# Sixty-two more unread TensorE products, of 128 columns, ahead of the transposes and values of units 1 to 3

## The chip, the cores and the metric

The kernel runs on one core of a Trainium2 chip. The metric is the device time of one execution in microseconds; lower is better. The times before are those of three runs.

## The reference

Sliding-window attention over 8 batches and 8 heads (576 positions, 64 numbers a head, window of 32 to each side), then a feed-forward layer with a quick gelu, all given and returned as float32:

```python
q, k, v: (8, 8, 576, 64);  w_in: (512, 2048);  w_out: (2048, 512)

scores = (1 / sqrt(64)) * q @ k.T
scores = where(abs(i - j) <= 32, scores, -1e9)
attn   = exp(scores - rowmax);  attn = attn / (rowsum + 1e-9)
x      = (attn @ v)            # heads side by side: (4608, 512)
h      = x @ w_in
out    = (h * sigmoid(1.702 * h)) @ w_out      # (4608, 512)
```

## The kernel before

The 4608 tokens are cut into 36 *units* of 128 tokens and 9 *tiles* of 512 (four units). For a unit, `scores` multiplies the transposed q and k of all heads into two banks of PSUM, ScalarE takes the exponential into `p`, VectorE multiplies it by the band mask (`band`), `values` multiplies `p` by v with a column of ones beside it into `pv`, and `norm` divides by the sum that this column gives and writes `x`. `x_T` and `x_T2` transpose `x` on TensorE, for one unit and for two, and copy the result into `xT`, the moving operand of layer one. Layer one (`h`) is 16 groups of products a tile with a gelu each, layer two (`o`) follows; from tile 1 on both use seven products of sums of blocks in place of eight, whose sums VectorE makes (`x_sums`, line 354, and `g_sums`).

Everything is recorded in an order written out by hand, one queue an engine; the engines wait for one another by semaphores that the framework sets from the tiles used. `opening` holds the order for the first tiles. It begins with tile 0: q and k of the first batch come in two parts and are transposed on TensorE by `T_first`, then units 0 and 1 go through scores, band, values and norm, and their `x` is transposed by two calls of `x_T` (lines 614 and 616). The second part of k is transposed (line 617), layer one of the first half of tile 0 begins (`layer1_plain`, lines 625, 627, 632 and 633, eight products of 256 columns each), with the second part of q and the scores of units 2 and 3 in between. `self.do(gelus)` records four gelus on ScalarE. Then come the bands, the values and norms of units 2 and 3 (lines 636 to 641) and `x_T2(2, "A", dve)`, line 642, which transposes both.

PSUM banks go by tags: "t" is a pair of banks, "A", "B", "C", "E", "LA" and "LB" one each. A new use of a tag waits until the readers of its last use are done.

`keep_busy(n, tag, cols=256)` records `n` products of an all-zero tile with itself, of `cols` columns, into the bank `tag`; no instruction reads the result. Each product is two TensorE instructions, a weight load and the product. In the profile they are `junk<-idle`. The kernel calls it in six places of the opening, with 256 columns, two of them (lines 613 and 615) ahead of the transposes of units 0 and 1. In the profile every product that `mm` records has line L70.

Of the kernel before, what the change touches and what calls it, by code (L numbers as in the profile page):

```python
# [26 lines left out]
class _Kernel:  # L27
# [534 lines left out]
    def opening(self):  # L562

        nc, dve, act, pool = self.nc, self.nc.vector, self.nc.scalar, self.nc.gpsimd
        self.setup()
        dve.memset(self.idle, 0.0)
        dve.memset(self.spark, 0.0)
        for t in self.ve:
            dve.memset(t[:, :, self.D:], 1.0)
        self.load_first("k", 0)  # L570
        self.load_first("q", 0)
        make_identity(nc, self.ident)
        act.activation(self.spark, self.spark, AF.Exp)
        for u in (0, 1, 2):
            self.load_v(u)
        self.load_w1(0)
        self.setup_mask()
        self.load_first("k", 1)
        self.load_first("q", 1)
        self.cut_mask()  # L580
        self.load_w1(1)
        self.load_v(3)
        self.load_v(4)
        self.load_w1(2)
        self.load_four("k")
        self.load_four("q")
        self.load_w1(3)
        dve.tensor_copy(self.identh, self.ident)
        self.keep_busy(20, "E")
        self.T_first("k", 0, "AC", (dve, act))  # L590
        self.keep_busy(6, "E")
        self.T_first("q", 0, ("LA", "LB"), (dve, act))
        self.keep_busy(4, "E")
        for u in (5, 6):
            self.load_v(u)
        self.load_w2(0)
        for u in (7, 8):
            self.load_v(u)
        for c in (1, 2, 3):
            self.load_w2(c)  # L600
        self.load_kq("k", 8)
        self.scores(0, "t")
        self.scores(1, "AC")
        self.odd_v(0, dve)
        self.odd_v(1, dve)
        self.keep_busy(10, "E")
        self.band(0)
        self.band(1)
        self.values(0, "t")
        self.values(1, "AC")  # L610
        self.norm(0)
        self.norm(1)
        self.keep_busy(6, "E")
        self.x_T(0, "LA", act)
        self.keep_busy(4, "E")
        self.x_T(1, "LB", act)
        self.T_first("k", 1, "AC", (dve, dve))
        h, n, gelus = [], [0], []

        def l1(half, *ds):  # L620
            for d in ds:
                self.layer1_plain(0, d, half, h[n[0] % len(h)])
                n[0] += 1

        self.layer1_plain(0, 0, 0, "B", gelus)
        self.T_first("q", 1, ("LA", "LB"), (dve, act))
        self.layer1_plain(0, 1, 0, "E", gelus)
        self.odd_v(2, dve)
        self.odd_v(3, dve)
        h[:] = ["LB", "B", "E"]  # L630
        self.scores(2, "t")
        self.scores(3, "AC")
        self.layer1_plain(0, 2, 0, "LA", gelus)
        self.layer1_plain(0, 3, 0, "LB", gelus)
        self.do(gelus)
        self.band(2)
        self.band(3)
        self.values(2, "t")
        self.norm(2)
        self.values(3, "AC")  # L640
        self.norm(3)
        self.x_T2(2, "A", dve)
        l1(0, 4)
        dve.tensor_copy(self.k_first, self.kT[0][:, :, 0:64])
        dve.tensor_copy(self.v_first, self.ve[0][0:64])
        for u in (8, 9, 10, 11):
            self.fetch(u)
        l1(1, 0, 1)
        halo = self.kT[4]
        self.T_four("k", "AC", (dve, dve))  # L650
        dve.tensor_copy(self.kT[4][:, :, 0:64], halo)
        l1(1, 2, 3)
        l1(0, 5)
        self.T_four("q", "AC", (dve, act))
        l1(1, 4, 5)
        self.odd_v(4, dve)
        self.scores(4, "t")
        self.scores(5, "AC")
        for i in (3, 1, 2, 4):
            self.w1_sums((i,), 0)  # L660
        self.odd_v(5, dve)
        for d, tag in ((6, "B"), (7, "E")):
            self.layer1_plain(0, d, 0, tag, gelus)
        self.do(self.l2, 3)
        self.scores(6, "t")
        self.do(self.l2, 3)
        self.scores(7, "AC")
        self.do(gelus)
        self.do(self.l2, 2)
        self.band(4)  # L670
        self.band(5)
        self.odd_v(6, dve)
        self.odd_v(7, dve)
        self.band(6)
        self.values(4, "t")
        self.norm(4)
        self.band(7)
        self.values(5, "AC")
        self.norm(5)
        self.do(self.l2, 8)  # L680
        self.values(6, "t")
        self.norm(6)
        self.values(7, "AC")
        self.norm(7)
        h[:] = "BE"
        n[0] = 0
        for i in (3, 1):
            self.w1_sums((i,), 1)
        l1(1, 6, 7)
        self.x_T2(4, "A", act)  # L690
        self.do(self.l2, 4)
        self.x_T2(6, "t", dve)
        self.do(self.l2, 4)
# [214 lines left out]
```

## Time and profile before

| what | value |
|---|---|
| median of three runs | 288.69 us (288.52 to 289.27) |
| span of the profiled execution, first to last instruction | 287.4 us |
| the median less the span | 1.3 us |
| instructions | 9107 |
| TensorE busy, products and their weight loads | 274.7 us, 3762 of each |
| granted TensorE clock, mean | 1.000 |
| DMA read and written | 36.83 MB, 9.44 MB |

The execution that was profiled has no time of its own among the three runs; what is worked out from its rows is set against its span, and the 1.3 us outside the span are taken as fixed. Busy time of TensorE counts products as they overlap; two products that follow each other closely each show the full time from start to end, so the step from one start to the next is what a product costs. A line of the timeline gives the start, the time from the first start to the last end, engine, line, operation, output and inputs, the count, and in brackets the idle time ahead of it and what ended it. In a row of the table of stretches, the numbers are: stretch, its length, busy time and count of products (PE), of weight loads (PEld), then of VectorE, ScalarE and GpSimd, the granted clock, the busy share of the DMA engines and the GB/s.

### The profile page before, as it was taken

The numbers are of one execution on the slowest core, as the hardware profiler recorded it, in microseconds if no ns is written. First come the engines' busy times: TensorE is split into PE (matmuls) and PEld (weight loads), VectorE is DVE, ScalarE is ACT, GpSimd is POOL, SyncE is SP. The second block draws the span as 40 slices with busy tenths as digits, with TensorE's granted clock in tenths as the row PEclk, the third lists the DMA queues.
The fourth block names the chain that finished last, engine by engine and source line by source line (L and its number), as shares of the span: only waits on it lengthen the run. The fifth ranks groups of instructions, "written<-read, shape, count | busy, mean of one in ns | idle before, by whom it ended". The sixth has DMA issues, their size and how long they took to land.

```text
span 287.4 us, 9107 instructions
## 1 busy us (share of the span) xinstructions
PE 274.7 (96%) x3762; PEld 227.1 (79%) x3762; DVE 216.9 (75%) x501; ACT 194.0 (68%) x340; POOL 127.3 (44%) x192
## 2 busy tenths in 40 slices
PE   7878999999999997999999999999999999999995
PEld 5666857776777885888788888888888888888884
DVE  1756898897887975798779887988797878946731
ACT  2455784789787767676967696679668965558421
POOL 8964448798599746456345826360210000000000
PEclk9999999999999999999999999999999999999999
DMA  8999999999999999999999999998432150401023
GB/s 94 186 192 197 184 204 156 190 116 140 168 141 148 175 142 173 138 203 144 188 97 181 161 168 105 173 135 146 95 77 45 69 112 0 94 2 73 2 92 130
DMA packets 148074, 37.63 MB, mean 131 GB/s; under 512 B 134976, under 2 KB 143680, under 8 KB 148032
## 3 DMA queue, kind: packets, MB, share of 16 engines
q0 software_dynamic: 104464, 18.42, 92.3%
q1 hardware_dynamic: 43120, 18.10, 36.0%
q8 instruction: 29, 0.48, 0.7%
q10 hardware_dynamic: 448, 0.52, 0.6%
q14 instruction: 13, 0.11, 0.1%
HBM read 36.83 MB, written 9.44 MB: 161 GB/s over the span
## 4 chain that ended last, share of the span: by engine, by line
PE 81%; DMA 5%; DVE 5%; ACT 3%; POOL 2%; issue 2%; DVEq 0%; ACTq 0%; POOLq 0%
PE h L70 38%; PE o L70 34%; PE pv L70 3%; DMA xT<-x 3%; PE sc L70 2%; DMA kq<-in_k_dram 2%; DVE x L294 2%; ACT p L256 1%; PE tp L322 1%; POOL ve L199 1%; ACT L256 1%; DVE p L264 1%; PE tp L189 1%; PE tp L232 1%; ACT g L419 1%
## 5 line engine op out<-in xcount | busy, mean ns | idle before, releaser
L419 ACT ACTIVATE g<-h 128x512 f16<-128x512 f32 x128 | 72.1, 598 | 35.8 <-PE h L70 35.0
L70 PEld LDWEIGHTS <-g 128*128 128x128 f16 x576 | 54.4, 98 | 11.4 <-issue 1.8
L70 PEld LDWEIGHTS <-a 128*128 128x128 f16 x512 | 49.1, 97 | 12.7 <-DVE xs L354 2.1
L70 PE MATMUL h<-xs,a 128*128 128x256 f16 x384 | 57.6, 272 | 1.2 <-DVE xs L354 0.9
L70 PE MATMUL o<-w,g 128*128 128x256 f16 (+1 forms) x320 | 55.3, 294 | 0.9 <-issue 0.8
L70 PEld LDWEIGHTS <-w 128*128 128x128 f16 x512 | 49.1, 98 | 7.8 <-issue 1.2
L70 PE MATMUL h<-xT,w 128*128 128x256 f16 x384 | 54.0, 273 | 1.1 <-issue 1.0
L199 POOL DMA_DIRECT2D ve<-in_v_dram x40 | 34.0, 855 | 40.7 <-issue 33.7
L70 PEld LDWEIGHTS <-gs 128*128 128x128 f16 x384 | 36.8, 98 | 5.2 <-issue 0.4
L256 ACT ACTIVATE p<-sc 128x512 bf16<-128x512 f32 x72 | 36.6, 619 | 3.2 <-PE sc L70 3.2
L70 PE MATMUL o<-b,gs 128*128 128x256 f16 x256 | 37.8, 273 | 1.0 <-issue 0.5
L70 PE MATMUL o<-b,g 128*128 128x256 f16 x256 | 37.3, 273 | 0.0
L432 DVE TENSOR_TENSOR h<-h,s 128x512 f32<-128x512 f32 x32 | 22.3, 698 | 18.2 <-PE h L70 18.2
L131 POOL DMA_DIRECT2D qst<-in_q_dram x35 | 28.1, 805 | 5.5 <-DMA w<-in_moe_w_out_dram 3.2
L131 POOL DMA_DIRECT2D kst<-in_k_dram x31 | 26.4, 854 | 8.5 <-DMA ve<-in_v_dram 2.6
L67 ACT COPY h<-h 128x512 f32<-128x512 f32 x32 | 18.6, 581 | 16.6 <-PE h L70 16.2
L294 DVE TENSOR_TENSOR x<-pv,rec 128x256 f16<-128x256 f32 (+1 forms) x53 | 27.6, 520 | 1.8
L438 DVE TENSOR_TENSOR h<-h,s 128x512 f32<-128x512 f32 x32 | 22.4, 700 | 5.1 <-PE h L70 4.6
L264 DVE TENSOR_TENSOR p<-p,mask 128x1024 bf16<-128x1024 bf16 x36 | 24.6, 685 | 0.9 <-ACT p L256 0.8
L209 POOL COPY vo<-ve 64x264 int32<-64x264 int32 x28 | 13.4, 480 | 24.9 <-PE pv L70 23.8
L67 ACT COPY s<-h 128x512 f32<-128x512 f32 x32 | 19.1, 596 | 3.0 <-PE h L70 1.8
L70 PE MATMUL h<-xs,w 128*128 128x256 f16 x128 | 19.2, 273 | 0.0
(85 smaller groups left out, 361.1 us busy)
## 6 DMA issues: line engine op xcount, KB each, us to landing
out_dram<-o_sb SPq DMA_DIRECT2D x33, 256.0 KB, 3.9
ve<-in_v_dram POOLq DMA_DIRECT2D x32, 128.0 KB, 6.3
kst<-in_k_dram POOLq DMA_DIRECT2D x25, 128.0 KB, 6.8
qst<-in_q_dram POOLq DMA_DIRECT2D x21, 128.0 KB, 6.1
w<-in_moe_w_in_dram POOLq DMA_DIRECT2D x4, 512.0 KB, 8.9
w<-in_moe_w_out_dram POOLq DMA_DIRECT2D x4, 512.0 KB, 13.4
qst<-in_q_dram POOLq DMA_DIRECT2D x7, 96.0 KB, 5.5
kq<-in_q_dram POOLq DMA_DIRECT2D x2, 256.0 KB, 5.9
```

The source lines that it names most:

```text
L67: (eng.copy if eng is self.nc.scalar else eng.tensor_copy)(out, in_)
L70: self.nc.tensor.matmul(out, lhsT, rhs, start=start, stop=stop, skip_group_check=True)
L131: self.nc.gpsimd.dma_start(t[off:off + n], src[b, :, s:s + n, :].rearrange("h s d -> s h d"))
L189: self.nc.tensor.transpose(tp[64 * (h % 2):64 * (h % 2) + 64, h // 2, j, :], src[:, 4 * i + h, j, :], self.ident)
L199: self.nc.gpsimd.dma_start(t[off:off + n, :, :self.D], self.v[b, :, s:s + n, :].rearrange("h s d -> s h d"))
L209: eng.tensor_copy(words(vo[64:128]), words(self.ve[u % 9][64:128]))
L256: self.nc.scalar.activation(p[:, eo].rearrange("k h s -> k (h s)"), sc[eo], AF.Exp, scale=self.scale)
L264: (eng or self.nc.vector).tensor_mul(pv, pv, msk.to_broadcast([128, 8, 2, SQ]))
L294: dve.tensor_mul(x[:, 4 * at:4 * (at + n), :].rearrange("p (b h) d -> p b h d", b=n), acc[:, :, :, :D], r.to_broadcast([128, n, 4, D]))
L419: act.activation(g[:, f, 256 * half:256 * half + 256], bank.rearrange("p (i n) -> p i n", i=2), AF.Gelu_apprx_sigmoid)
L432: dve.tensor_add(e, b, s7)
L438: dve.tensor_add(c, b, s7)
```

## The change

Two calls of `keep_busy` ahead of the transposes of units 0 and 1 take 12 and 8 products of 128 columns in place of 6 and 4 of 256. Three calls are new: 12 products ahead of the transposes of the second part of k, 20 ahead of the values of unit 2, into the banks of tag "t", and 20 ahead of the transposes of units 2 and 3, into bank "B". That is 72 products of 128 columns in place of 10 of 256. Nothing that is read changes.

```diff
         self.norm(0)
         self.norm(1)
-        self.keep_busy(6, "E")
+        self.keep_busy(12, "E", 128)
         self.x_T(0, "LA", act)
-        self.keep_busy(4, "E")
+        self.keep_busy(8, "E", 128)
         self.x_T(1, "LB", act)
+        self.keep_busy(12, "E", 128)
         self.T_first("k", 1, "AC", (dve, dve))
...
         self.do(gelus)
         self.band(2)
         self.band(3)
+        self.keep_busy(20, "t", 128)
         self.values(2, "t")
         self.norm(2)
         self.values(3, "AC")
         self.norm(3)
+        self.keep_busy(20, "B", 128)
         self.x_T2(2, "A", dve)
         l1(0, 4)
```

## The prediction

> **What bounds the kernel now.** I read the page's busy row first, then the chain of waits of the whole span, then TensorE's waits in the opening, then the timeline of the stretch that the change touches.
>
> ```profile
> PE 274.7 (96%) x3762; PEld 227.1 (79%) x3762; DVE 216.9 (75%) x501; ACT 194.0 (68%) x340; POOL 127.3 (44%) x192
> PE 81%; DMA 5%; DVE 5%; ACT 3%; POOL 2%; issue 2%; DVEq 0%; ACTq 0%; POOLq 0%
> ```
>
> TensorE is busy for 96% of the span and carries 81% of the chain. From 24 us on hardly any idle time stands between its products, so microseconds lost in the opening should be paid at the end too. TensorE's waits up to 30 us are these, the largest first:
>
> ```profile
> PE junk L70 <- DVE spark L567: 1.3, 1, 1.3
> PE tp L322 <- DVE x L294: 1.1, 1, 1.1
> PE h L70 <- issue: 1.0, 1, 1.0
> PE pv L70 <- DVE p L264: 1.0, 2, 0.5
> PE tp L168 <- DMA kq<-in_k_dram: 0.9, 2, 0.5
> ```
>
> Only 1.1 us (the transposes of units 2 and 3) and half of the last row (the second k transposes) are waits that the added products can stand in. The third row, "issue", is 1.0 us in which TensorE waited for nothing that the profile shows. TensorE's timeline, with the mask products and exponentials that feed the values of units 2 and 3 (the values lines left out):
>
> ```profile
> 1.27 4.26 PE L70 MATMUL junk<-idle 128*128 128x256 bf16 x20 [1.27 <-DVE spark L567]
> ...
> 12.47 0.83 PE L70 MATMUL junk<-idle 128*128 128x256 bf16 x6
> 13.14 0.39 PE L310 MATMUL tp<-identh,x 128*128 128x128 f16 x4
> 13.36 0.60 PE L70 MATMUL junk<-idle 128*128 128x256 bf16 x4
> 13.80 0.52 PE L310 MATMUL tp<-identh,x 128*128 128x128 f16 x4
> 14.86 0.71 PE L168 MATMUL tp<-ident,kq 64*64 64x64 bf16 x32 [0.54 <-DMA kq<-in_k_dram]
> 15.51 1.05 PE L70 MATMUL h<-xT,w 128*128 128x256 f16 x8
> ...
> 18.11 0.70 PE L70 MATMUL sc<-kq 64*64 64x64 bf16 x48
> 18.74 1.48 PE L70 MATMUL h<-xT,w 128*128 128x256 f16 x12
> 21.24 0.60 PE L70 MATMUL h<-xT,w 128*128 128x256 f16 x4 [1.02 <-issue]
> 21.77 0.22 PE L70 MATMUL pv<-ve,p 128*64 128x65 bf16 x1
> ...
> 23.82 0.83 PE L322 MATMUL tp<-identh,x 128*128 128x128 f16 x8 [1.08 <-DVE x L294]
> 18.60 2.07 ACT L256 ACTIVATE p<-sc 128x512 bf16<-128x512 f32 x4 [0.78 <-PE sc L70]
> 20.96 1.27 DVE L264 TENSOR_TENSOR p<-p,mask 128x1024 bf16<-128x1024 bf16 x2
> ```
>
> Twelve of sixteen layer-one products run, then TensorE stands from 20.22 to 21.24 in the middle of a group, its data and bank there. I read this as TensorE out of instructions, for this reason. The counts of products and weight loads up to that stall and up to the two later "issue" stalls of 0.8 and 0.5 us (109.65 and 139.52 us), in the table of stretches; the counts are in the third and fourth columns' brackets:
>
> ```profile
> 0.00:15.07 15.07, 11.93 (x223) 8.96 (x224) 6.57 (x26) 6.00 (x10) 13.52 (x29) 1.00 1.24 143
> 0.00:18.48 18.48, 15.34 (x327) 11.74 (x329) 8.84 (x30) 6.59 (x11) 15.14 (x31) 1.00 1.32 150
> 0.00:20.50 20.50, 17.08 (x350) 13.14 (x351) 9.51 (x33) 8.48 (x15) 16.38 (x33) 1.00 1.34 155
> 20.50:109.90 89.40, 85.52 (x1273) 65.25 (x1272) 73.42 (x157) 68.08 (x119) 63.59 (x87) 1.00 1.93 162
> 109.90:139.80 29.90, 28.03 (x382) 23.55 (x383) 23.44 (x55) 20.65 (x37) 17.06 (x25) 1.00 2.04 168
> 34.14:40.08 5.94, 5.71 (x147) 3.81 (x135) 5.60 (x13) 5.89 (x11) 2.82 (x4) 1.00 1.49 195
> 104.52:109.65 5.13, 5.13 (x130) 4.00 (x127) 4.06 (x10) 4.99 (x9) 4.20 (x6) 1.00 2.02 130
> ```
>
> First stall after 350 + 351 = 701; then 2545 to the second and 765 to the third, which is ten and three times 256 less 15 and 3; I put the missing few down to separate wait instructions in TensorE's list, which these columns leave out. So stalls come only at every 256th instruction. Within each such block one packet of queue 8 is read, and in the block before the first stall it falls between 18.7 and 19.8 us:
>
> ```profile
> q8 instruction: 1, 0.02, 5.7%
> ```
>
> That block begins near count 701 - 256 = 445, at about 15.07 us (447 begun by then); the next may start only at 21.24. So from beginning one block to being allowed into the next takes about 21.24 - 15.07 = 6.17 us here. A block used up sooner ends in a stall: the one from 104.52 was used in 5.13 us and was followed by 0.8 us of idling (5.94 in all). [...]
>
> **The change part by part.** A 128-column product costs 55 ns: four transposes of that width start at 13.14 and the next work at 13.36. One of 256 columns costs (13.14 - 12.47) / 6 = 112 ns. Only TensorE's list grows, by 124 instructions (62 products and their loads); the other engines' lists and all DMA issues stand in the same order.
>
> *Ahead of unit 0's and unit 1's transposes:* 12 narrow for 6 wide, 12 x 55 = 0.66 against 0.67 us; 8 for 4, 0.44 against 0.44. Nothing; 20 more instructions.
>
> *Ahead of the second k transposes:* 12 x 55 = 0.66 us. Unit 1's transposes leave TensorE at about 14.16, the k rows arrive at 14.86: 0.70 us of cover. Nothing, with 0.04 us to spare, 24 more instructions. Without that cover it costs 0.66.
>
> *The stall.* These 44 instructions stand before it. The block that begins at count 445 now begins inside the twelve new products, at about 14.27 instead of 15.07; adding 6.17, the next block is allowed at 20.4. But the 701st instruction is now what was the 657th, in the middle of unit 3's scores, which TensorE reaches at 18.48 (327 + 329 = 656 begun). So TensorE stands from about 18.5 to 20.4, 1.9 us, in place of 1.2 (from 20.06, where the next product was due at 109 ns steps, to 21.24). Bounds for the restart: 18.5 if the reading of blocks is wrong or the block comes at once, 21.24 if the fetch keeps its old hour because the DMA queues are what delays it. I take 20.4, the row's own round trip.
>
> *Ahead of the values of unit 2:* 20 x 55 = 1.1 us. Now the rest: from 18.48 to unit 2's values the old trace has 0.26 of scores, 1.32 for twelve products and 0.53 for four, 2.11 us. 20.4 + 2.11 + 1.1 = 23.6, against 21.77: **+1.85 us**. The wait that these products could have stood in, for the mask product (the first ends near 21.6), is already over by 22.5. Behind them queue the values of both units, then reciprocals and normalisations on VectorE, the transposes and layer one. Unit 3's exponentials come after the stall, near 20.7 to 21.8, and its mask product by 22.5, still ahead of 23.6; the gelus slip by 1 us and are done by 25.2, before their banks are wanted near 26.3.
>
> *Ahead of units 2's and 3's transposes:* 20 x 55 = 1.1 us in the wait of 1.08 us, which moves along with the values: about nothing (0 to 0.1), since bank B's gelu is over by then. Without that cover, 1.1.
>
> *Later.* With 124 more instructions every later block begins 124 earlier in the program. The stall at 139.52 is in TensorE's own run of work, so its going gives -0.5. The one at 109.65 gives nothing: the chain through it is a DMA transpose, and TensorE waits for its result 2 us later anyhow:
>
> ```profile
> 103.43 8.78 DMA xT<-x
> PE h L70 <- DVE xs L354: 0.9, 1, 0.9
> ```
>
> New stalls: at the moved places the shortest block I find after the opening is that of 34.14 to 40.08, 5.94 us (the row's 282 counts products in flight at the edges), against 5.7 to 6.2: 0 to 0.3. I take 0.
>
> *Sum:* +1.85 - 0.5 = +1.3 us. The profiled span is 287.4 us and the median of the timed runs 288.69, so 1.3 us lie outside the span and are left as they are: 288.69 + 1.3 = **290.0 us**. About 0.3%, 0.9 us, is what a measurement of this kernel can tell from no change.
>
> **The rivals.** *No stall in the opening* (0.16): the next block is there by 18.5. Then layer one ends near 20.6, the twenty products fill the wait for the mask product until about 21.7, and nothing is lost; with the 0.5 won later, 288.2, and 287.4 if the 0.8 us counts too. For it: the block of 104.52 came after 5.94 us, so the trip is not fixed at 6.17. Against it: three stalls, all on the 256 grid. It decides if the round trip is below 18.75 - 14.27 = 4.5 us.
>
> *Bare products* (0.12): the stall is no matter of blocks and stays as large, 1.0 to 1.2 us, at the same product, and nothing changes later; the twenty before unit 2's values lie open: +1.1, 289.8.
>
> *The fetch keeps its hour* (0.13): restart at 21.24, so 21.24 + 2.11 + 1.1 - 21.77 = +2.7, less 0.5: 290.9.
>
> *Swallowed downstream* (0.12): loads and DMA transposes do not wait for the shifted TensorE, so the 8.78 us transpose gets shorter against it, by up to the 0.9 us wait: 289.1.
>
> *Clock* (0.02): the products keep TensorE's clock up and layer one runs faster. The first twenty wide ones took 4.26 / 20 = 213 ns each, later ones 112; the granted clock reads 1.00 in every row, and layer one steps at 109 ns on both sides of its stalls. After the longest wait, 1.08 us, nothing is slow, so there is nothing to gain: 288.7 less nearly zero. [...]
>
> **How the numbers follow.** The forecast has 0.45, with a range of its own of 289.4 to 290.6 (0.3 us either way for the round trip and for a new stall). The range reaches to the first rival's 288.2 and past the late fetch's 290.9: 288.1 to 291.0. Slower by over 0.3% (over 289.56): nearly all of the forecast, 0.41, bare products 0.11, late fetch 0.13: 0.65. Within: the swallowed case, most of the first rival, the forecast's low edge: 0.25. Faster: the first rival with both stalls gone, and the clock: 0.10.
>
> **What would show it.** Right: an "issue" wait of about 1.9 us that begins inside unit 3's scores near 18.5, unit 2's values near 23.6, no "issue" wait at 110 and 140, and layer one after the transposes beginning near 26.3 instead of 24.49. Wrong: the stall still between layer one's products, or none before 24 us, or unit 2's values at 21.8 with the twenty products ahead of them in a wait; also steps of layer one under 109 ns, or new "issue" waits after 30 us that take back the 0.5.

## The result, and the profile after

The changed kernel takes 290.38 us (median; 288.83 to 295.29) against 289.37 us (287.27 to 292.2) of the kernel before, run beside it. The ratio is 1.0052, with a 95% interval of 1.0026 to 1.0077: slower by 0.52%, about 1.5 us; the medians differ by 1.0 us. A second set of runs gave 290.47 against 289.60 us, 0.9 us more, ratio 1.0031 (0.9998 to 1.0063), which by itself does not exclude no change. The forecast was 290.0 us and +1.3; the kernel before now came out 0.7 us above the 288.69 us that the forecast started from, so the differences are to be compared, not the times.

The first profile of the changed kernel was taken in a disturbed execution (295.29 us, granted clock 0.994 over the span), so only its opening is read; everything else is from the second profile of the same kernel, with a span of 291.3 us, which at 293.06 us is itself 2.6 us above the median of its set. The page's busy row:

```profile
PE 281.0 (96%) x3824; PEld 232.4 (80%) x3824; DVE 217.2 (75%) x501; ACT 194.0 (67%) x340; POOL 126.7 (43%) x192
```

TensorE's waits over the whole span (in total, times, the longest; others left out):

```profile
PE h L70 <- DVE xs L354: 1.9, 2, 1.1
PE sc L70 <- issue: 0.9, 1, 0.9
...
PE tp L322 <- DVE x L294: 0.2, 1, 0.2
```

TensorE has 62 products more, as the change says. The wait for the normalised rows of units 2 and 3 is 0.2 us in place of 1.1. The "issue" wait has left layer one (`h`) for the scores (`sc`), and the two later "issue" waits on `o` are gone. New and large is the wait for the sums of tile 3 and the next, 1.9 us in place of 0.9. TensorE's timeline of the stretch that the change touches (the values lines left out, but for the first):

```profile
14.99 0.84 PE L70 MATMUL junk<-idle 128*128 128x128 bf16 x12
...
16.80 0.83 PE L70 MATMUL junk<-idle 128*128 128x128 bf16 x12
17.56 0.72 PE L168 MATMUL tp<-ident,kq 64*64 64x64 bf16 x32
...
20.81 0.59 PE L70 MATMUL sc<-kq 64*64 64x64 bf16 x38
22.30 0.31 PE L70 MATMUL sc<-kq 64*64 64x64 bf16 x10 [0.89 <-issue]
22.54 1.92 PE L70 MATMUL h<-xT,w 128*128 128x256 f16 x16
24.30 1.28 PE L70 MATMUL junk<-idle 128*128 128x128 bf16 x20
...
25.64 0.19 PE L70 MATMUL pv<-ve,p 128*64 128x65 bf16 x1
26.27 1.29 PE L70 MATMUL junk<-idle 128*128 128x128 bf16 x20
27.67 0.83 PE L322 MATMUL tp<-identh,x 128*128 128x128 f16 x8
28.33 0.38 PE L70 MATMUL h<-xT,w 128*128 128x256 f16 x2
```

Everything here stands some 2.4 us later than in the profile of before, and that is no effect of the change: it is there already at the first scores, 11.06 us against 8.68, ahead of the first changed line. The reason is in the last section. So openings are compared by one stretch, from the first of the second k transposes to the first layer-one product after units 2 and 3. It is 24.49 - 14.86 = 9.63 us before and 28.33 - 17.56 = 10.77 us after (10.71 in the first profile).

The stall is where the forecast put it, inside unit 3's scores: after 38 of the 48 products of two units. It is shorter, 0.9 us (0.8 in the first profile) against 1.9. The stretch up to it counts as before, 350 products and 351 loads, in both profiles of the changed kernel, the second below:

```profile
0.00:22.20 22.20, 19.31 (x350) 14.48 (x351) 10.78 (x33) 7.48 (x13) 17.63 (x35) 1.00 1.30 152
```

### The profile page after: what moved, and what is told of

Read it like the earlier page. It is cut to its first block, busy times and chain, and to the rows that moved or that the text cites. A ratio compares the mean times of both kernels' runs of the same rounds, so it can differ in the third digit from the quotient of the medians.

```text
span 293.6 us, 9230 instructions
## 1 busy us (share of the span) xinstructions
PE 282.4 (96%) x3824; PEld 233.3 (79%) x3824; DVE 218.2 (74%) x501; ACT 193.9 (66%) x340; POOL 126.3 (43%) x192
## 4 chain that ended last, share of the span: by engine, by line
PE 84%; DVE 5%; DMA 5%; ACT 3%; issue 2%; DVEq 0%; ACTq 0%; POOLq 0%
PE h L70 38%; PE o L70 34%; PE pv L70 3%; DMA xT<-x 3%; PE sc L70 3%; DVE x L294 2%; PE junk L70 2%; DMA kq<-in_k_dram 2%; ACT p L256 1%; PE tp L168 1%; PE tp L322 1%; ACT L256 1%; DVE p L264 1%; PE tp L189 1%; PE tp L232 1%
## 5 line engine op out<-in xcount | busy, mean ns | idle before, releaser
L70 PE MATMUL h<-xs,a 128*128 128x256 f16 x384 | 58.3, 274 | 3.2 <-DVE xs L354 3.1
```

The lines of the kernel that those rows point to most:

```text
L70: self.nc.tensor.matmul(out, lhsT, rhs, start=start, stop=stop, skip_group_check=True)
```

## The experiments

The theory, read from the counts of the kernel before (stops after 701 products and loads, then 2545 and 765 more): TensorE stops at every 256th instruction if it used up the block before too fast, as the one from 104.52, used in 5.13 us and followed by 0.8 us of idling; the change moves such a stop into unit 3's scores, which leaves the products ahead of unit 2's values without a wait to stand in, and it also moves the later stops. The first rival: the stall belongs to a product of layer one, its data or its bank, and the products simply lie open. The second: the products stand in waits, and something later sets the time.

### The changed kernel once more

No edit.

> The changed kernel as it is, for more times and a profile of an ordinary run. Block theory (TensorE stands at every 256th instruction when the next block is not there): one issue wait of 0.8 to 1.9 us inside unit 3's scores, none at 110 and 140 us, 1.0 to 1.9 us over the kernel before. Bare-products rival (the stall is tied to a product, not to a count): an issue wait of 1.0 us between layer one's products, +1.1 us.

The times and rows are those above; +0.9 us by the medians is just under the 1.0 to 1.9 expected. The place of the stall (0.9 us in the scores) and the absence of "issue" waits near 110 and 140 us speak for the theory; a wait between layer one's products, as the rival has it, is not there.

### Forty more instructions, and forty fewer, at the same TensorE time

```diff
-        self.keep_busy(20, "E")
+        self.keep_busy(40, "E", 128)
```

> The kernel before with its very first 20 unread products of 256 columns cut into 40 of 128: the same TensorE time, 40 more instructions before the first data arrives, nothing else. Block theory: the issue wait moves from layer one's products into unit 3's scores (0.7 to 1.5 us there), without a change of unit 2's values beyond 0.5 us; time within 0.5 us of before. Rival (stall tied to that layer-one product, its data or bank): the wait stays after the twelfth product, 1.0 us.

Measured: 288.72 us against 289.60, ratio 0.9966 (0.9930 to 1.0002). Its TensorE waits up to 30 us:

```profile
PE junk L70 <- DVE spark L567: 1.3, 1, 1.3
PE tp L322 <- DVE x L294: 0.9, 1, 0.9
PE h L70 <- ACT g L390: 0.4, 1, 0.4
PE pv L70 <- DVE p L264: 0.4, 1, 0.4
PE tp L168 <- DMA kq<-in_k_dram: 0.3, 1, 0.3
```

The wait in layer one is gone, though not one of its products was touched. But it did not move into the scores; there is no stop at all. The trace offers a reason. The packet of queue 8, which the profile names "instruction", ends at 19.13 us here; in the eleven profiles that do stop at this count, TensorE goes on 1.3 to 1.7 us after the end of that packet (1.49 in the kernel before, 1.45 in the first profile of the changed kernel), which here would be 20.4 to 20.8 us, and TensorE comes to the 701st instruction at 20.5 us. So by this estimate, if that packet is the next block, the block was there about when it was wanted. This opening steps at 213 ns a product until some 13.5 us (last section), but that is not the reason by itself: three other profiles have such an opening and stop. The rival's wait after the twelfth product is refuted; the expected size of the wait was a miss, and so was the time, 0.9 us under the kernel before, though its interval reaches no change.

```diff
-        self.keep_busy(20, "E")
+        self.keep_busy(10, "E", 512)
...
-        self.keep_busy(6, "E")
+        self.keep_busy(3, "E", 512)
...
-        self.keep_busy(4, "E")
+        self.keep_busy(2, "E", 512)
...
-        self.keep_busy(10, "E")
+        self.keep_busy(5, "E", 512)
```

> The kernel before with its first four calls of unread products (20, 6, 4 and 10 of 256 columns) made of half as many of 512: the same TensorE time, 40 fewer instructions. Block theory: the 701st instruction falls into unit 3's values, which wait for their mask product anyhow, so no issue wait is left in layer one and at most 0.3 us before the values; the 110 and 140 us waits go too. Time 0 to 0.7 us under before. Rival (stall tied to that layer-one product): an issue wait of 1.0 us where it was, time as before.

Measured: 290.49 us against 289.60, ratio 1.0001 (0.9965 to 1.0037). TensorE's largest waits:

```profile
PE pv L70 <- DVE p L264: 2.2, 4, 1.0
PE h L70 <- DVE xs L354: 1.6, 2, 1.4
PE h L70 <- issue: 1.2, 1, 1.2
```

As expected no "issue" wait is left before the values of unit 2; a wait of 1.0 us for the mask product stands in its place, and the stretch is 9.70 us against 9.63. So in the kernel before, the stall costs next to nothing: the mask product ends only when it is over. The time did not fall, which was a miss: the one "issue" wait on `h` is at 84.6 us, a new stop of 1.2 us, after 1240 products and 1241 loads. That is 1780 more than 701, seven times 256 less 12 that the theory puts down to separate wait instructions.

### The first three edits alone

```diff
-        self.keep_busy(6, "E")
+        self.keep_busy(12, "E", 128)
         self.x_T(0, "LA", act)
-        self.keep_busy(4, "E")
+        self.keep_busy(8, "E", 128)
         self.x_T(1, "LB", act)
+        self.keep_busy(12, "E", 128)
```

> The kernel before with only the change's first three edits (12, 8 and 12 products of 128 columns; 44 more instructions before the second k transposes). Theory: they cost nothing where they stand but move the block's end into unit 3's scores: issue wait of about 1.4 us there (0.6 to 0.9 if the opening runs at half the step rate), the stretch from the second k transposes to layer one 9.7 to 10.4 us against 9.6; later issue waits near 110 and 140 us shrink or go: 0 to 0.7 us slower than before. Rival (moving the block's end is harmless): stretch 9.6 us.

Measured: 289.09 us against 289.49, ratio 1.0003 (0.9972 to 1.0034). Its timeline:

```profile
14.35 0.83 PE L70 MATMUL junk<-idle 128*128 128x128 bf16 x12
15.12 0.72 PE L168 MATMUL tp<-ident,kq 64*64 64x64 bf16 x32
...
18.36 0.59 PE L70 MATMUL sc<-kq 64*64 64x64 bf16 x38
20.12 0.31 PE L70 MATMUL sc<-kq 64*64 64x64 bf16 x10 [1.16 <-issue]
20.36 1.92 PE L70 MATMUL h<-xT,w 128*128 128x256 f16 x16
24.27 0.51 PE L322 MATMUL tp<-identh,x 128*128 128x128 f16 x6 [1.35 <-DVE x L294]
```

Here the opening has the speed of the profile of before, and the stop is in the scores again, 1.2 us. The stretch is 9.83 us: the moved stop costs 0.2, at the low end of what was expected. The rows ahead of it show another thing: the k transposes no longer wait for their data. They start at 15.12, when the twelve products are through, while the k rows were there by 14.57 to 14.86 in four kernels without these products whose opening was as quick. By these the twelve are not covered in full: an estimated 0.3 to 0.5 us. The cover varies: in the kernel with the longer first call (below) the rows came only at 15.64. The waits at 110 and 140 us are gone, but there is a new "issue" wait of 0.7 us near 82 us.

### The products ahead of unit 2's values, alone and taken away

```diff
+        self.keep_busy(20, "t", 128)
         self.values(2, "t")
```

> The kernel before with only the 20 products of 128 columns ahead of unit 2's values. Block theory: the 701st instruction is where it was, so the 1.0 us issue wait stays between layer one's products; the 20 products then lie open, +1.1 us at the values of unit 2; from there every block begins 40 instructions earlier, so the waits near 110 and 140 us move or shrink: +0.6 to +1.1 us in all. Rival (the products stand in a wait): +0.

Measured: 289.17 us against 289.60, ratio 0.9971 (0.9945 to 0.9997). The rows of this stretch:

```profile
21.16 0.60 PE L70 MATMUL h<-xT,w 128*128 128x256 f16 x4 [1.03 <-issue]
21.59 1.28 PE L70 MATMUL junk<-idle 128*128 128x128 bf16 x20
22.93 0.19 PE L70 MATMUL pv<-ve,p 128*64 128x65 bf16 x1
24.95 0.83 PE L322 MATMUL tp<-identh,x 128*128 128x128 f16 x8 [1.33 <-DVE x L294]
25.62 0.60 PE L70 MATMUL h<-xT,w 128*128 128x256 f16 x4
```

The stall is unmoved at 1.0 us, and the twenty products lie open: values start 22.93 - 21.16 = 1.77 us after the restart in place of 0.53, and the stretch is 25.62 - 14.65 = 10.97 us, +1.34. So far as expected. The time is not: it came out 0.3% lower, where 0.2 to 0.4% more was expected. The profiled span is 288.0 against 287.4 us, but the timed runs say the reverse. A kernel further down helps to read this: it has the same 40 instructions more, but with its twenty products in a wait, and it is 0.35% faster than the kernel before (288.40 us). So 40 more instructions seem to win about what the open products lose.

```diff
-        self.keep_busy(20, "t", 128)
         self.values(2, "t")
```

> The changed kernel without its 20 products ahead of unit 2's values. Theory (they lie open, since the block stall has used up the wait for the mask product): the issue wait stays inside unit 3's scores at 0.8 to 1.9 us, and the stretch from the second k transposes to the first layer-one product after units 2 and 3 shrinks from 10.7 us to 9.6 us; 1.1 us faster than the changed kernel if nothing downstream takes it back. Rival (they stand in a wait): that stretch stays at 10.7 us.

Measured: 289.45 us, against 290.38 and 290.47 of the changed kernel: 1.0 us faster, as expected (ratio to the kernel before 0.9992, 0.9955 to 1.0028). Its timeline:

```profile
18.41 0.59 PE L70 MATMUL sc<-kq 64*64 64x64 bf16 x38
20.41 0.31 PE L70 MATMUL sc<-kq 64*64 64x64 bf16 x10 [1.40 <-issue]
20.66 1.92 PE L70 MATMUL h<-xT,w 128*128 128x256 f16 x16
23.77 1.28 PE L70 MATMUL junk<-idle 128*128 128x128 bf16 x20 [0.56 <-ACT g L390]
24.89 0.61 PE L322 MATMUL tp<-identh,x 128*128 128x128 f16 x8
```

The restart at 20.41 meets the forecast's 20.4 by chance: the two other kernels that carry the twelve products and had a quick opening restart at 20.12 and 20.15. The stretch is 10.18 us, longer than the 9.6 expected, since the last row but one shows a cover that is gone: without the twenty, the products into bank B come before ScalarE's gelu has read that bank, wait 0.56 us for it, and the transposes come late.

### The products ahead of the transposes of units 2 and 3, taken away and alone

```diff
-        self.keep_busy(20, "B", 128)
         self.x_T2(2, "A", dve)
```

> The changed kernel without its 20 products ahead of the transposes of units 2 and 3. Theory (they stand in the wait for the normalised rows): the stretch from the second k transposes to the first layer-one product after units 2 and 3 stays at 10.7 us, with a wait of about 1.1 us before those transposes; time as the changed kernel within 0.5 us. Rival (they cost too): the stretch shrinks by up to 1.1 us.

Measured: 290.72 us, as the changed kernel (ratio to the kernel before 1.0025, 0.9987 to 1.0062). The transposes wait 1.3 us where they stood behind products, and the stretch is 10.50 us against 10.71 to 10.77; the stall is 0.6 us in place of 0.8 to 0.9, which is that difference. So these products cost nothing there.

This kernel and the one without the products ahead of unit 2's values were timed in the same set of runs and have the same number of instructions, 84 more than the kernel before, so that by the theory all later blocks end alike. The one that keeps the open products takes 290.72 us, the one that keeps the covered ones 289.45: 1.3 us. Their ratios to the kernel before, 1.0025 and 0.9992, have intervals that overlap, so the sign is better known than the size.

```diff
+        self.keep_busy(20, "B", 128)
         self.x_T2(2, "A", dve)
```

> The kernel before with only the 20 products ahead of the transposes of units 2 and 3. Theory: they stand in the 1.1 us wait, so the stretch from the second k transposes to layer one stays at 9.6 us, the issue wait between layer one's products stays at 1.0 us, and 40 more instructions take the issue waits near 110 and 140 us away: 0.5 to 1.3 us faster than before. Rival (later block ends do not matter, the DMA transposes set the time there): time as before within 0.3 us.

Measured: 288.40 us against 289.49, ratio 0.9965 (0.9935 to 0.9995): faster than the kernel before by 0.35%, 1.0 us, and by its median 2 us under the changed kernel. In its timeline the products stand in the wait:

```profile
20.95 0.60 PE L70 MATMUL h<-xT,w 128*128 128x256 f16 x4 [1.02 <-issue]
22.51 1.29 PE L70 MATMUL junk<-idle 128*128 128x128 bf16 x20
23.64 0.77 PE L322 MATMUL tp<-identh,x 128*128 128x128 f16 x8
24.25 0.60 PE L70 MATMUL h<-xT,w 128*128 128x256 f16 x4
```

The stretch is 24.25 - 14.57 = 9.68 us, and between 100 and 150 us TensorE waits for two things only:

```profile
PE h L70 <- DVE xs L354: 0.3, 1, 0.3
PE sc L70 <- issue: 0.2, 1, 0.2
```

against 0.9 and 1.3 us of the kernel before. The likely cause is that 40 more instructions move the ends of the later blocks: the two other kernels with 40 more, put in at other places, have ratios of 0.9971 and 0.9966. It is not shown in full, since the rows are of one execution, which at 287.44 us lies 1.0 us under the median of its kernel.

### The same TensorE time with fewer instructions

The changed kernel with its products of 128 columns as a quarter as many of 512, and the four earlier calls as in the run with forty fewer.

```diff
-        self.keep_busy(20, "t", 128)
+        self.keep_busy(5, "t", 512)
...
-        self.keep_busy(20, "B", 128)
+        self.keep_busy(5, "B", 512)
```

> The changed kernel with its products of 128 columns as a quarter as many of 512, and the four earlier calls as half as many of 512: the same TensorE time in every call, 24 instructions fewer than the kernel before instead of 124 more. Block theory: the 701st instruction falls into unit 2's values; no issue wait in unit 3's scores, the products ahead of unit 2's values end near when the mask product does, and the stretch from the second k transposes to layer one shrinks from 10.7 us to 9.6 to 9.8; 1 us faster than the changed kernel. Rival (TensorE time of the products is the cost, wherever the blocks fall): the stretch stays at 10.7 us.

Measured: 290.77 us against 289.67, ratio 1.0052 (1.0011 to 1.0092). The stretch is 9.73 us, as expected: with the stop out of the scores, the same TensorE time costs 0.1 us in place of 1.1. The total was a miss. The profile has a new stop of 1.0 us in the scores at 84 us, the row below, and 1.2 us of waiting for the sums later on:

```profile
84.48 0.25 PE L70 MATMUL sc<-qT,kT 64*64 64x128 bf16 x5 [1.02 <-issue]
```

Together these waits are as long as the 1.3 and 0.9 us of the kernel before, so they do not explain why this kernel is 0.5% slower than it; that stays open.

### A longer first call

```diff
-        self.keep_busy(20, "E")
+        self.keep_busy(26, "E")
```

> The kernel before with 26 unread products in its very first call instead of 20, nothing else. Some profiles run that opening at half the step rate (213 ns a product of 256 columns until 13.4 us), others change to 109 ns at 5.1 us; the first k transposes come after a gap of 0.3 to 0.45 us. Theory (that gap decides whether TensorE's clock comes up early): with the gap filled, products step at 109 ns from 7 us at the latest, the second k transposes begin by 15.3 us instead of 14.9 or 17.4; the spread of the times shrinks and the median drops by 0.5 to 1 us. Rival (the clock's change comes by its own beat): one opening in some is as slow as before, median plus 0 to 0.5 us.

Measured: 289.65 us against 289.67, ratio 1.0004 (0.9970 to 1.0038). The profile has the quick opening. The granted clock reads 1.00 in it (first 20.8 us) as in the slow one (first 22.2 us of the second profile of the changed kernel), so what the expectation puts down to the clock shows in the step alone. But the second k transposes begin at 15.64, after 0.8 us of waiting for the k rows, and not by 15.3 as expected; a later "issue" wait, near 110 us, is 1.6 us in place of 0.8. The median did not move, where 0.5 to 1 us less was expected. Whether the longer call keeps the opening quick in every execution is open: the three kernels with it were all quick when profiled, and of the eleven others seven.

The changed kernel with this call:

> The changed kernel with 26 products in its very first call instead of 20. Theory: the opening then steps at 109 ns as in the profile of before, TensorE uses up its block sooner, and the issue wait in unit 3's scores grows from 0.8 to 0.9 us to 1.2 to 1.9 us; the stretch from the second k transposes to layer one is 11.2 to 11.6 us. Rival (the prediction's 6.17 us round trip is too long): the wait stays at 0.8 to 1.0 us and the stretch at 10.7 us. The time falls by less than 1 us against the changed kernel.

Measured: 290.58 us against 289.49, ratio 1.0047 (1.0015 to 1.0079). This is the changed kernel with the quick opening:

```profile
15.29 0.71 PE L168 MATMUL tp<-ident,kq 64*64 64x64 bf16 x32
...
18.53 0.53 PE L70 MATMUL sc<-kq 64*64 64x64 bf16 x32
20.15 0.38 PE L70 MATMUL sc<-kq 64*64 64x64 bf16 x16 [1.09 <-issue]
```

The stall is 1.1 us and the stretch 10.96 us: between the theory's and the rival's numbers. The time did not fall against the changed kernel. Layer one after the transposes starts at 26.25 us; the forecast had 26.3, but 0.2 us of this is an opening that is later from its first scores on (8.87 against 8.68 us), ahead of the change.

### The covered products only

```diff
-        self.keep_busy(20, "E")
+        self.keep_busy(26, "E")
...
+        self.keep_busy(32, "B", 64)
         self.x_T2(2, "A", dve)
```

> The kernel before with 26 products in its very first call and 32 products of 64 columns ahead of the transposes of units 2 and 3, none ahead of unit 2's values: the clock up early, only covered products, and every block after the opening begins 76 instructions earlier, where the nearest short blocks are at 12 and 77 us. Theory: no issue wait over 0.5 us after 30 us, 1 us faster than the kernel before. Rival (later block ends do not matter): time as before within 0.3 us.

Measured: 288.82 us against 289.49, ratio 0.9975 (0.9943 to 1.0007): not told from no change, where 1 us less was expected, and not better than the twenty products alone. After 30 us its largest "issue" wait is 0.3 us, as expected.

## Why the prediction was right, point by point

*The total.* The forecast had the way and nearly the size: +1.3 us, against 0.9 to 1.5. Part of this is luck. Two of its terms were off in opposite ways, a third is not shown, and the rival of bare products, at +1.1 us, would have met the measured time as well. What speaks for the forecast's mechanism is the place of the stall, not the time.

*The bound.* That a delay of the opening is paid at the end is shown in sign and not in kind. For it: taking the open products from the changed kernel gives 1.0 us back, and in two pairs with equal numbers of instructions the kernel with the open products is the slower by its median, by 1.3 us (290.72 against 289.45) and by 0.7 (0.4 and 1.1 us under their own kernel before), with intervals that overlap in both. Against it: the kernel with the wide products has a stretch of 9.73 us and a ratio of 1.0052.

*The instruction blocks.* The grid of 256 is shown. In eleven of the fourteen profiles, with the change's calls whole, in part or not at all, the first "issue" wait comes after 350 products and 351 loads, whatever product that is. The kernels with 40 and with 24 instructions fewer have none there; that count falls into their values. The one with 40 more comes to that count at 20.5 us, 1.4 us after the end of its packet. In the kernel before, counted with TensorE's 39 separate instructions, 36 of them on semaphores, 705 instructions have begun ahead of the first stop and 4033 ahead of the third, 13 times 256 more; 29 packets of queue 8 are read in its span, 16 KB each, for 7563 such instructions, 29.5 times 256. Counted in this way, all 22 "issue" waits of the fourteen profiles stand at whole multiples of 256 from one another, once the four products that the trace of the wide kernel lacks are added. In the eleven, TensorE goes on 1.3 to 1.7 us after the end of the packet of queue 8 that falls in the block (kernel before: packet from 18.75 to 19.75 us, restart at 21.24; changed kernel: 19.62 to 20.57, restart at 22.02 in the first profile, and 19.92 to 21.00, restart at 22.30 in the second). That this packet brings the next block is a reading of these times; no run moved the packet by itself. The rival that tied the stall to a layer-one product is out, and so is a stall that only happens to stand at this count.

*The stall's size* was mis-sized: 1.9 us predicted, 0.8 to 0.9 in the two profiles of the changed kernel, 1.1 with the quick opening, 1.2 and 1.4 in the kernels with the first three edits. Some 0.2 us of the gap are a matter of measure: the forecast counted from when the next product was due (1.2 us for the stall of before, which the profile gives as 1.0). From the start of the last product to the next start TensorE stands 1.3 us in the kernel before and 1.3 to 1.6 us in the three quick ones, so the moved stop adds 0 to 0.3 us and not the 0.7 of the forecast. The stretch agrees: 10.97 us with the twenty open products and the stop in its old place, 10.77 and 10.96 with the whole change. The block's round trip is not fixed at 6.17 us. With the block beginning inside the twelve products, at about 14.5 us, it is 5.6 and 5.9 us in the kernels with the first three edits (restarts at 20.12 and 20.41), and 5.3 in the first profile of the changed kernel (16.7 to 22.0). The forecast's limit for its first rival, 4.5 us, was also too long: TensorE reaches the stop at 18.48 us in the forecast's own reckoning, and 18.48 - 14.27 is 4.2.

*The products ahead of the second k transposes:* no cost was predicted, with 0.04 us to spare. The spare was not there; they cost an estimated 0.3 to 0.5 us when the opening is quick. This, by luck, made up for much of what the stall lacked: with the quick opening the layer-one products begin at 26.25, or 26.05 without the 0.2 us by which that opening is late, against 24.49 + 1.85 = 26.34 predicted.

*The products ahead of unit 2's values:* 1.1 us predicted, 1.3 measured. The values write the bank that the products wrote. In the run with these products alone the first of the values starts at 22.93, 0.28 us after the last product started, where the products follow each other in 0.056. Where the next work goes to another bank the 0.2 us are not there: in the kernel with the last call alone the transposes, into bank A, start at 23.64, 0.06 us after the last product into bank B. A product takes 0.22 us from start to end, so the 0.2 are, by the author's estimate, TensorE waiting for its own last product.

*The products ahead of units 2's and 3's transposes:* free, as predicted, in the changed kernel and alone. Only with the stop moved and the products ahead of unit 2's values taken away do they wait, 0.56 us for bank B.

*Later.* The "issue" waits at 110 and 140 us went, as predicted, and -0.5 us was taken for it. Its size stays open. From the end of the stretch to the end of the span, the changed kernel takes 291.3 - 28.33 = 263.0 us and the kernel before 287.4 - 24.49 = 262.9, so in this profile nothing is won: the wait for the sums behind the DMA transposes grew from 0.9 to 1.9 us. But that execution is the one 2.6 us above its median. In the changed kernel with the longer first call, profiled at 289.85 us, 0.7 us under its median, it is 288.1 - 26.25 = 261.9, 1.1 us less than before, and in the kernel with the last call alone 285.7 - 24.25 = 261.5, with that wait at 0.3, in an execution that was 1.0 us under the median. One execution of each does not tell the term. The chain through the wait holds a DMA transpose in all that were read, of 8.78 us before, 8.41 in the changed kernel and 8.39 with the last call alone. What sets its start, and so whether removed stops are won or waited away, was not tried.

*The clock.* No gain from it showed, as predicted: layer one steps at 109 to 110 ns with and without the products.

*The rivals.* None took the place of the forecast, but the one of a delay swallowed downstream is out only as a whole: of the 1.3 us by which the open products lengthen the stretch at 40 more instructions, the medians show 0.7.

*What lies outside the span.* The 1.3 us that the forecast took for it is the difference of two executions: each timed run here is 1.7 us longer than its own span (289.49 against 287.8). The forecast's difference does not depend on it.

## What to carry to other kernels

An "issue" wait in the middle of a group of products, with its data there, is worth counting: here such waits stood at multiples of 256 instructions of TensorE, and added instructions moved them, for better or worse (44 more took the first from layer one into the scores, at 1.2 in place of 1.0 us). Filler is free only while the wait it stands in is still there when the engine arrives; here a stop of TensorE ahead of it, of 1.0 us in its old place and 0.8 to 1.1 in its new one, had used that wait up, and twenty products lay open at 1.3 us. Where filler wrote the bank of the work behind it, that work started 0.28 us after the last product, and 0.06 us where it did not, so another bank was the better place.

## What the runs showed of the hardware that was not expected

The opening has two speeds, and kernels whose instructions are the same up to 12 us show the one or the other. In the profile of before, unread products of 256 columns step at 213 ns until 5.1 us, and the next ones, from 6.67 us on, at 109 to 112 ns; in the ten quick profiles the change comes at 3.8 us at the earliest and always ahead of the products at 6.7 to 7.3 us. In four of the fourteen profiles, both of the changed kernel among them, the step stays at 213 ns until 13.5 to 13.9 us. The second profile of the changed kernel shows it in the ten products at 12.06, 2.08 us in place of 1.27:

```profile
12.06 2.08 PE L70 MATMUL junk<-idle 128*128 128x256 bf16 x10
```

The granted clock reads 1.00 in both cases. The slow step costs some 2.4 us by 15 us. In the profile of before the change of step comes after 3.8 us from the first product on; the late ones come after some 12 us of products with waits of 0.3 to 0.7 us among them. What sets it was not shown.

A kernel with more unread work can be faster than one with less: with 20 more products that stand in a wait it took 1.0 us less (ratio 0.9965), and the change in fewer instructions was 0.5% slower than the kernel before (1.0052) though its stretch was only 0.1 us longer.
